# The last 64 tokens of local queries and keys: two full transpositions in place of four half ones

## The chip, the cores and the metric

The kernel runs on one core of a Trainium2 chip. The metric is the device time of one execution in microseconds. Five engines work beside each other, each through its own list of instructions: TensorE (PE for the matmuls, PEld for the weight loads that go before them), VectorE (DVE), ScalarE (ACT), GpSimd (POOL) and SyncE (SP), which here only starts DMA transfers. A transposition on TensorE is a matmul against an identity: the data is loaded as the weights, the identity is streamed, and the result lands in PSUM, from where ACT copies it to SBUF.

## The reference

Attention over 8 batches of 8 heads, 576 tokens of 64 values each, then a mixture of 8 experts over the 4608 tokens. Only the first step is touched by the change.

```python
scores = scale * np.matmul(q, k.transpose(0, 1, 3, 2))
rel = pos[:, None] - pos[None, :]
mask_local = (rel >= 0) & (rel < 32)                       # heads 0 to 3
mask_strided = (rel >= 0) & (rel % 32 == 0)                # heads 4 to 7
attn = softmax(where(mask, scores, -1e9))                  # per head
x = (attn @ v)  ->  (4608, 512)
e = argmax(x @ w_gate);  y = relu(x @ w1[e]) @ w2[e] * gate
```

## The kernel before, in words

The attention goes batch by batch. Heads 4 to 7 ("s", strided) and heads 0 to 3 ("l", local) alternate in a pipeline of 40 steps, five to a batch: `ch` lists them, and the loop over `n` writes the instructions of one step for every engine. Each engine runs its instructions in the order in which this loop wrote them. In step `n` the loads of the next batch are issued on SP, the transpositions for step `n + 3` are written (`tr`), the scores of step `n + 1` (`qks`, `qkl`), the softmax of step `n` and the products with the values of step `n - 2` (`avs`, `avl`).

The local queries and keys of a batch are loaded by `load_l`, 128 tokens at a time: `jj` runs over 0 to 4, and 576 = 4 x 128 + 64, so that the fifth piece has only 64 tokens. A piece is one DMA for q (tile `ql`) and one for k (tile `kl`): tokens on the partitions, the four heads one behind the other in the free dimension. `tl` transposes a piece: two heads (2 x 64 values) at a time, so four transpositions, two of `ql` (line 191) and two of `kl` (line 193), into one PSUM tile `t`; one ACT copy (line 194) brings them into `QK[b % 2]`, where the scores are taken from. For the fifth piece the four transpositions have 64 rows of tokens as input and 64 columns of output.

The order around it: `tl(b, 4)` stands at the start of a step, directly behind the value products `avl` (line 346) and ahead of the strided scores `qks` (lines 226, 231) and of the strided queries of the next batch (`ts`, line 203). On SP the loads of one batch come in the order q and k of the strided heads (`load_s`, lines 87 and 88, tiles `qs` and `ks`), local q and k (line 103), strided values (`load_vs`, line 93), local values (`load_vl`, line 112). Between them stand the stores of finished rows to `xrows` (line 381), each of which waits for ACT's copy into `xr`. For batches 0 and 1 nothing is stored yet. The DMAs of SP take turns on eight completion semaphores (DMAHW0 to DMAHW7 in the lists below): each DMA first waits until the one eight places ahead of it has landed. Names in the trace: buffers that lie inside other tiles show as `w` (strided keys and values of odd batches), `xg` (local values of odd batches) and `x` (`QK` of odd batches).

Of the kernel before, what the change touches and what calls it, by code (L numbers as in the profile page):

```python
# [12 lines left out]
AF = mybir.ActivationFunctionType  # L13
# [5 lines left out]
B, H, S, D = 8, 8, 576, 64  # L19
ST = 32  # L20
# [19 lines left out]
def kernel(ctx, tc, q, k, v, w_gate, w1, w2, out):  # L40
    nc = tc.nc
    V, A, G, T = nc.vector, nc.scalar, nc.gpsimd, nc.tensor
# [17 lines left out]
    ql, kl, vl, qs, ks, vs = {}, {}, {}, {}, {}, {}  # L60

    QK = [p0.tile([128, 2, 2, ST + S], F32, name="qk"),
          XA[:, :4 * (ST + S)].rearrange("p (w h s) -> p w h s", w=2, h=2)]
# [16 lines left out]
    def base(t, b, h):  # L80
        return t.offset + (b * H + h) * S * D
# [15 lines left out]
    def load_l(b, jjs=range(5)):  # L97
        for jj in jjs:
            for nm, src, dst in (("ql", q, ql), ("kl", k, kl)):
                if jj == 0:  # L100
                    dst[b] = ld.tile([128, 5, 4, D], F32, name=nm)
                n = 128 if jj < 4 else 64
                nc.sync.dma_start(dst[b][:n, jj], bass.AP(tensor=src.tensor, offset=base(src, b, 0) + jj * 128 * D,
                                                          ap=[[D, n], [S * D, 4], [1, D]]))

    def load_vl(b):
        t = VL[b % 2]
# [19 lines left out]
    ident = keep.tile([128, 128], F32)  # L127
    V.tensor_scalar(ident, jp, 0.0, None, op0=OP.is_equal)
    identb = const.tile([128, 128], BF)
    V.tensor_copy(identb, ident)  # L130
    load_s(0)
    load_l(0, (0, 1))

    rowq = const.tile([128, 1], F32)
# [50 lines left out]
    QTS, PS, PL, PT, OL, XS, XL, RL = ({} for _ in range(8))  # L185

    def tl(b, jj):
        n = 128 if jj < 4 else 64
        p = ps.tile([128, 4, 128], F32, name="t", bufs=3)
        for a in range(2):  # L190
            T.transpose(p[:, a, :n], ql[b][:n, jj, 2 * a:2 * a + 2, :], ident[:n, :n])  # L191
        for a in range(2):
            T.transpose(p[:, 2 + a, :n], kl[b][:n, jj, 2 * a:2 * a + 2, :], ident[:n, :n])
        A.activation(QK[b % 2].rearrange("p w h s -> p (w h) s")[:, :, ST + 128 * jj:ST + 128 * jj + n], p[:, :, :n], AF.Copy)
        yield

    def ts(b, w, x):
# [388 lines left out]
    src = keep.tile([TM, NC], I32, name="src")  # L586
# [88 lines left out]
    def tr(n):  # L675
        if not 0 <= n < N: return
        kd, b, i = ch[n]
        if n % 5 == 0:
            yield from ts(b, 1, 0)
            yield from ts(b, 1, 1)  # L680
            yield from ts_end(b)
        elif kd == "l":
            for jj in ((0, 1), (2, 3), (4,))[i]:
                yield from tl(b, jj)
            if i == 2 and b + 1 < B:
                yield from ts(b + 1, 0, 0)
                yield from ts(b + 1, 0, 1)
# [11 lines left out]
    def batch(n, d, f):  # L699
        if (n - d) % 5 == 4 and 0 <= (n - d) // 5 < B:  # L700
            return f((n - d) // 5)

    load_l(0, (2, 3, 4))
    load_vs(0)
    load_vl(0)
    for n in range(-1, N + 3):
# [5 lines left out]
        bb, m = n // 5 + 1, n % 5  # L712
# [3 lines left out]
        if bb < B:  # L716
            if m == 0 and n >= 0:
                if n == 0:
                    load_s(1)
                load_l(bb, (0, 1))  # L720
                if n == 0:
                    load_prev(0)
            if m == 1:
                load_l(bb, (2, 3, 4))
            if m == 2:
                load_vs(bb)
            if m == 3:
                load_vl(bb)
                if bb + 1 < B and n > 0:
                    load_s(bb + 1)  # L730
            if m == 4 and n > 0:
                load_prev(bb)
# [8 lines left out]
        if n == 1:  # L741
            nc.sync.dma_start(wg[:, :, :8], bass.AP(tensor=w_gate.tensor, offset=w_gate.offset,
                                                    ap=[[8, 128], [1024, 4], [1, 8]]))
# [54 lines left out]
    b = B - 1  # L798
# [298 lines left out]
    with tc.If(total > 0):  # L1097
# [10 lines left out]
        for e in range(E):  # L1108
            nc.sync.dma_start(f1, w1[e].rearrange("(c p) f -> p c f", p=128))
            nc.sync.dma_start(f2, w2[e].rearrange("(c p) d -> p c d", p=128))  # L1110
            n = nc.values_load(lvi[0:1, E + e:E + e + 1], min_val=0, max_val=NTOK)
# [56 lines left out]
```

## Time and profile before

| what | value |
|---|---|
| median of the runs shown (lowest, highest) | 663.3 us (662.58, 672.38), 3 runs |
| the profiled execution | 660.2 us, its span 658.4 us |
| PE busy over the span | 612.1 us (93%), 7502 matmuls |
| PEld busy | 542.1 us (82%) |
| DVE, ACT, POOL busy | 376.2, 323.6, 206.3 us |
| share of the last chain of work | PE 57%, issue 15%, SP's queue 8%, DVE 8%, ACT 6%, DMA 3% |

The profile is of one execution; 1.8 us of its 660.2 us lie outside the span from the first to the last instruction. The chain of work that ended last is followed back from the end, at each step to what released it; "issue" is time for which the profile shows no waited-for work. The attention takes the first 200 us or so, the experts the rest.

### The profile page before, as it was taken

What the parts mean: (1) busy time and instruction counts of PE and PEld (TensorE: products, weight loads), DVE (VectorE), ACT (ScalarE), POOL (GpSimd) and SP (SyncE); (2) the same over time, 40 slices, a digit from 0 to 9 for tenths busy, and PEclk for the clock granted to TensorE, in tenths of its full rate; (3) what the DMA queues carried; (4) which work ended last, traced back from release to release, by engine and by line L of the source; (5) the groups of instructions that cost most, each with busy time, mean ns of one, the idle gap of its engine ahead of it and who ended that gap; (6) DMA issues with size and microseconds to landing.
All of it is one profiled execution on the core that took longest, in us unless ns stands there. A gap on an engine that the chain in (4) does not pass through costs nothing.

```text
span 658.4 us, 18975 instructions
## 1 busy us (share of the span) xinstructions
PE 612.1 (93%) x7502; PEld 542.1 (82%) x7502; DVE 376.2 (57%) x834; ACT 323.6 (49%) x647; POOL 206.3 (31%) x347
## 2 busy tenths in 40 slices
PE   6689999988987889999999999999999999999995
PEld 4467676766755768999899999999999999999994
DVE  5767889878898653765445544644462752544200
ACT  6457766866764342544543543643642742534311
POOL 0222256436445681504304203403301600110212
PEclk9689999999997999999999999999999999999998
DMA  8997798879555277658978678868467867453111
GB/s 189 185 233 195 194 229 208 203 191 223 136 187 167 84 265 148 209 109 173 323 126 202 226 143 177 310 120 213 156 160 126 283 196 127 159 150 71 49 37 58
DMA packets 237955, 114.24 MB, mean 174 GB/s; under 512 B 209053, under 2 KB 211101, under 8 KB 237728
## 3 DMA queue, kind: packets, MB, share of 16 engines
q1 hardware_dynamic: 230096, 89.70, 56.9%
q0 software_dynamic: 7632, 22.03, 10.5%
q8 instruction: 79, 1.29, 0.9%
q14 instruction: 148, 1.21, 0.6%
HBM read 74.47 MB, written 21.83 MB: 146 GB/s over the span
## 4 chain that ended last, share of the span: by engine, by line
PE 57%; issue 15%; SPq 8%; DVE 8%; ACT 6%; DMA 3%; POOL 1%; POOLq 0%; ACTq 0%; DVEq 0%
PE h L642 6%; PE h L643 6%; PE h L644 6%; SPq L611 4%; PE y L918 3%; PE y L917 3%; PE y L919 3%; SPq L941 3%; PE o L346 2%; PE t L191 2%; PE o L275 2%; PE sc L298 2%; PE t L203 2%; PE t L328 2%; PE sc L231 1%
## 5 line engine op out<-in xcount | busy, mean ns | idle before, releaser
L649 DVE SCALAR_TENSOR_TENSOR h1l<-h,h1h 128x256 fp32r<-128x256 f32 (+3 forms) x64 | 32.5, 507 | 90.3 <-ACT h1h L648 85.4
L642 PE MATMUL h<-x,w1h 128*128 128x256 f32 (+3 forms) x256 | 81.0, 316 | 1.2 <-ACT yo L666 1.2
L644 PE MATMUL h<-x,w1l 128*128 128x256 f32 (+3 forms) x256 | 80.8, 316 | 0.0
L643 PE MATMUL h<-x,w1h 128*128 128x256 f32 (+3 forms) x256 | 80.8, 316 | 0.0
L917 PE MATMUL y<-h1h,w 128*128 128x256 f32 (+4 forms) x256 | 79.4, 310 | 1.4 <-ACT yt L924 1.4
L918 PE MATMUL y<-h1l,w 128*128 128x256 f32 (+4 forms) x256 | 79.5, 310 | 0.1
L919 PE MATMUL y<-h1h,w 128*128 128x256 f32 (+4 forms) x256 | 79.2, 309 | 0.0
L905 POOL DMA_INDIRECT out_dram<-yo,idx x16 | 15.8, 990 | 181.3 <-ACT yo L666 181.0
L642 PE MATMUL h<-x0h,w1h 128*128 128x256 f32 x224 | 63.5, 284 | 0.4 <-DVE h0l L649 0.4
L643 PE MATMUL h<-x0l,w1h 128*128 128x256 f32 x224 | 63.3, 283 | 0.0
L644 PE MATMUL h<-x0h,w1l 128*128 128x256 f32 x224 | 63.3, 283 | 0.0
L603 POOL DMA_INDIRECT xg<-xrows,src x48 | 52.9, 1101 | 30.0 <-issue 12.5
L905 POOL DMA_INDIRECT out_dram<-yq,idx x32 | 36.2, 1130 | 79.1 <-ACT yq L945 54.8
L648 ACT ACTIVATE h1h<-h 128x256 fp32r<-128x256 f32 (+3 forms) x64 | 28.5, 451 | 63.9 <-PE h L644 52.1
L575 DVE TENSOR_TENSOR w1l<-stg,w1h 128x1024 fp32r<-128x1024 f32 x32 | 37.8, 1227 | 33.0 <-ACT w1h L574 11.6
L649 DVE SCALAR_TENSOR_TENSOR h0l<-h,h0h 128x256 fp32r<-128x256 f32 x56 | 22.8, 420 | 49.8 <-issue 25.5
L642 PEld LDWEIGHTS h<-x,w1h 128*128 128x128 f32 x256 | 48.0, 188 | 2.0 <-ACT yo L666 1.7
L917 PEld LDWEIGHTS y<-h1h,w 128*128 128x128 f32 x256 | 48.1, 188 | 1.7 <-ACT yt L924 1.6
L918 PEld LDWEIGHTS y<-h1l,w 128*128 128x128 f32 x256 | 48.1, 188 | 0.4 <-DVE h1l L649 0.3
L643 PEld LDWEIGHTS h<-x,w1h 128*128 128x128 f32 x256 | 48.0, 188 | 0.3
L919 PEld LDWEIGHTS y<-h1h,w 128*128 128x128 f32 x256 | 48.2, 188 | 0.1
L644 PEld LDWEIGHTS h<-x,w1l 128*128 128x128 f32 x256 | 48.0, 188 | 0.0
(255 smaller groups left out, 1527.4 us busy)
## 6 DMA issues: line engine op xcount, KB each, us to landing
stg<-in_moe_w_dram SPq DMA_DIRECT2D x64, 512.0 KB
xr<-xg SPq DMA_DIRECT2D x112, 96.0 KB
xrows<-xr SPq DMA_DIRECT2D x16, 512.0 KB
yq<-yt SPq DMA_DIRECT2D x112, 64.0 KB
qs<-in_q_dram SPq DMA_DIRECT2D x8, 512.0 KB
ks<-in_k_dram SPq DMA_DIRECT2D x8, 512.0 KB
ql<-in_q_dram SPq DMA_DIRECT2D x32, 128.0 KB
kl<-in_k_dram SPq DMA_DIRECT2D x32, 128.0 KB
```

Source lines behind the costliest of these rows:

```text
L575: V.tensor_tensor(l[:, i], t, h[:, i].bitcast(F32), op=OP.subtract)
L603: G.indirect_dma_start(out=XG[t], out_offset=None, in_=x_out[:rows, :], in_offset=bass.IndirectOffsetOnAxis(ap=src[:, NT * e + t:NT * e + ...
L611: nc.sync.dma_start(XR[ST * q:ST * q + ST, a], rows[ST * a:ST * a + ST, :, q])
L642: T.matmul(p, W1H[:, c, fs], x[0][:, c, :n], start=(c == 0), stop=False)
L643: T.matmul(p, W1H[:, c, fs], x[1][:, c, :n], start=False, stop=False)
L644: T.matmul(p, W1L[:, c, fs], x[0][:, c, :n], start=False, stop=(c == 3))
L648: A.activation(h[0][:, f, :n], p, AF.Relu)
L649: V.scalar_tensor_tensor(h[1][:, f, :n], p, 0.0, h[0][:, f, :n].bitcast(F32), op0=OP.max, op1=OP.subtract)
L905: i = G.indirect_dma_start(out=out, out_offset=bass.IndirectOffsetOnAxis(ap=idx[:r, c:c + 1], axis=0), in_=YO[t][:r], in_offset=None, boun ...
L917: T.matmul(p[:, :n], W2H[:, f, ds_], H1[0][:, f, cs], start=(f == 0), stop=False)
L918: T.matmul(p[:, :n], W2H[:, f, ds_], H1[1][:, f, cs], start=False, stop=False)
L919: T.matmul(p[:, :n], W2L[:, f, ds_], H1[0][:, f, cs], start=False, stop=(f == 7))
```

## The change

The fifth piece is laid out otherwise: heads 0 and 1 of the 64 tokens lie on partitions 0 to 63, heads 2 and 3 on partitions 64 to 127. So it takes two DMAs for q and two for k, 64 tokens by two heads each, instead of one and one with four heads, and one transposition of 128 rows for q and one for k instead of two and two of 64 rows. The result in PSUM has the same columns in the same order, now without gaps between them; the ACT copy reads the same number of elements. All else stays.

```diff
@@ load_l
-                n = 128 if jj < 4 else 64
-                nc.sync.dma_start(dst[b][:n, jj], bass.AP(tensor=src.tensor, offset=base(src, b, 0) + jj * 128 * D,
-                                                          ap=[[D, n], [S * D, 4], [1, D]]))
+                if jj < 4:
+                    nc.sync.dma_start(dst[b][:, jj], bass.AP(tensor=src.tensor, offset=base(src, b, 0) + jj * 128 * D,
+                                                             ap=[[D, 128], [S * D, 4], [1, D]]))
+                else:
+                    for a in range(2):
+                        nc.sync.dma_start(dst[b][64 * a:64 * a + 64, jj, :2],
+                                          bass.AP(tensor=src.tensor, offset=base(src, b, 2 * a) + jj * 128 * D,
+                                                  ap=[[D, 64], [S * D, 2], [1, D]]))
@@ tl
-        n = 128 if jj < 4 else 64
+        n, m = (128, 2) if jj < 4 else (64, 1)
         p = ps.tile([128, 4, 128], F32, name="t", bufs=3)
-        for a in range(2):
-            T.transpose(p[:, a, :n], ql[b][:n, jj, 2 * a:2 * a + 2, :], ident[:n, :n])
-        for a in range(2):
-            T.transpose(p[:, 2 + a, :n], kl[b][:n, jj, 2 * a:2 * a + 2, :], ident[:n, :n])
-        A.activation(QK[b % 2].rearrange("p w h s -> p (w h) s")[:, :, ST + 128 * jj:ST + 128 * jj + n], p[:, :, :n], AF.Copy)
+        for w, x in enumerate((ql, kl)):
+            for a in range(m):
+                T.transpose(p[:, m * w + a], x[b][:, jj, 2 * a:2 * a + 2, :], ident)
+        A.activation(QK[b % 2].rearrange("p w h s -> p (w h) s")[:, :, ST + 128 * jj:ST + 128 * jj + n],
+                     p[:, :2 * m].rearrange("p x (y t) -> p (x y) t", t=n), AF.Copy)
```

PE, the fifth piece of batch 1, before: it stands behind the value products of batch 0.

```order
L346 MATMUL o<-vl,ptl 32x64 x16
L191 MATMUL t<-ident,ql 128x64 [waits DMAHW2_49,Activation_49]
L191 MATMUL t<-ident,ql 128x64
L193 MATMUL t<-ident,kl 128x64 [waits DMAHW3_49]
L193 MATMUL t<-ident,kl 128x64
L226 LDWEIGHTS identb
```

The same place on PE after the change (line numbers are five or six higher).

```order
L351 MATMUL o<-vl,ptl 32x64 x16
L197 MATMUL t<-ident,ql 128x128 [waits DMAHW5_49,DMAHW4_49,Activation_49]
L197 MATMUL t<-ident,kl 128x128 [waits DMAHW7_49,DMAHW6_49]
L231 LDWEIGHTS identb
L231 MATMUL sc<-mks,identb 128x144 [waits DVE_49]
```

Two matmuls and their weight loads are gone, and each of the two that are left waits for two DMAs. Over the whole program PE's list is 16 matmuls shorter.

SP at the start of the program, before: from the fifth piece of batch 0 to the strided queries of batch 1, the last row.

```order
L103 DMA ql<-in_q_dram 64x4x64 [waits DMAHW4_49]
L103 DMA kl<-in_k_dram 64x4x64 [waits DMAHW5_49]
L93 DMA vs<-in_v_dram 18x4x512 [waits DMAHW6_49,DVE_49]
L93 DMA vs<-in_v_dram 18x4x512 [waits DMAHW7_49]
L93 DMA vs<-in_v_dram 18x4x512 [waits DMAHW0_49]
L93 DMA vs<-in_v_dram 18x4x512 [waits DMAHW1_49]
L112 DMA vl<-in_v_dram 32x18x64 [waits DMAHW2_49]
L112 DMA vl<-in_v_dram 32x18x64 [waits DMAHW3_49]
L112 DMA vl<-in_v_dram 32x18x64 [waits DMAHW4_49]
L112 DMA vl<-in_v_dram 32x18x64 [waits DMAHW5_49]
L87 DMA qs<-in_q_dram 128x1024 [waits DMAHW6_49]
```

The same stretch on SP after, up to the last of the local values; the strided queries of batch 1 follow with a wait on DMAHW0.

```order
L107 DMA ql<-in_q_dram 64x2x64 [waits DMAHW4_49]
L107 DMA ql<-in_q_dram 64x2x64 [waits DMAHW5_49]
L107 DMA kl<-in_k_dram 64x2x64 [waits DMAHW6_49]
L107 DMA kl<-in_k_dram 64x2x64 [waits DMAHW7_49]
L93 DMA vs<-in_v_dram 18x4x512 [waits DMAHW0_49,DVE_49]
L93 DMA vs<-in_v_dram 18x4x512 [waits DMAHW1_49]
L93 DMA vs<-in_v_dram 18x4x512 [waits DMAHW2_49]
L93 DMA vs<-in_v_dram 18x4x512 [waits DMAHW3_49]
L117 DMA vl<-in_v_dram 32x18x64 [waits DMAHW4_49]
L117 DMA vl<-in_v_dram 32x18x64 [waits DMAHW5_49]
L117 DMA vl<-in_v_dram 32x18x64 [waits DMAHW6_49]
L117 DMA vl<-in_v_dram 32x18x64 [waits DMAHW7_49]
```

Two transfers more stand ahead of the values, so the semaphore on which each later DMA waits belongs to a transfer two places further on. Two are added per batch, 16 in all, and 16 is twice around the eight semaphores: from the first load of expert weights on, SP's list and its waits are the same as before.

## Rows read from the trace of the kernel before

**Rows 1.** Busy time by stretch: length, engines (count), PE's clock, DMA share, GB/s.

```profile
0.00:200.00 200.00, 171.83 (x4565) 127.70 (x4567) 159.13 (x459) 135.23 (x297) 79.15 (x178) 0.96 0.82 197
240.00:659.00 419.00, 406.81 (x2620) 387.11 (x2618) 186.76 (x285) 173.47 (x322) 101.19 (x125) 0.99 0.64 165
```

**Rows 2.** What PE waited for, 0 to 200 us: total, times, longest.

```profile
PE t L203 <- DMA qs<-in_q_dram: 9.7, 2, 5.3
PE o L346 <- issue: 5.1, 6, 1.6
PE sc L231 <- issue: 2.8, 1, 2.8
```

**Rows 3.** Groups by form, 0 to 200 us: busy us, mean ns | idle before.

```profile
L191 PE MATMUL t<-ident,ql 64*128 64x64 f32 x16 | 2.7, 248 | 0.0
...
L193 PEld LDWEIGHTS t<-ident,kl 64*128 64x128 f32 x16 | 1.6, 139 | 0.0
```

**Rows 4.** Timeline of PE, 30 to 60 us: start, length of the merged group.

```profile
31.55 0.44 PE L191 MATMUL t<-ident,ql 128*128 128x128 f32 x2
31.82 0.38 PE L193 MATMUL t<-ident,kl 128*128 128x128 f32 x2
...
41.64 0.34 PE L191 MATMUL t<-ident,ql 64*128 64x64 f32 x2
...
42.03 0.30 PE L226 MATMUL sc<-mks,identb 128*128 128x144 bf16 x2
...
53.26 0.33 PE L218 MATMUL t<-ident,qs 128*128 128x128 f32 x1
...
53.63 0.72 PE L275 MATMUL o<-w,w 128*64 128x72 f32 x16
```

**Rows 5.** Semaphore instructions of PE's queue at lines 191 and 218: count, ns.

```profile
L191 PEldq EVENT_SEMAPHORE  x40: 51/51/332, 8.2 to 184.5; - x40
L218 PEldq EVENT_SEMAPHORE  x8: 51/51/51, 7.3 to 170.1; - x8
```

**Rows 6.** Timeline of SP's queue, 8 to 20 us.

```profile
9.00 0.77 SPq L103 DMA_DIRECT2D ql<-in_q_dram  x1
...
10.54 1.58 SPq L93 DMA_DIRECT2D vs<-in_v_dram  x4
```

**Rows 7.** The last chain within 0 to 30 us: start, length, what.

```profile
8.45 4.50 DMA kl<-in_k_dram
...
13.86 2.70 SPq L112
...
16.61 6.77 DMA qs<-in_q_dram
```

**Rows 8.** Busy time in a stretch of the start, columns as in rows 1.

```profile
11.00:14.00 3.00, 2.54 (x76) 2.00 (x76) 1.06 (x3) 2.91 (x7) 0.00 (x0) 1.00 0.60 128
```

**Rows 9.** Timeline of SP's queue, 20 to 200 us, loads for batches 1 and 2.

```profile
27.14 0.51 SPq L103 DMA_DIRECT2D kl<-in_k_dram  x1
27.69 0.61 SPq L103 DMA_DIRECT2D ql<-in_q_dram  x1
...
29.05 0.55 SPq L742 DMA_DIRECT2D wg<-in_moe_w_gate_dram  x1
...
35.35 1.76 SPq L87 DMA_DIRECT2D qs<-in_q_dram  x1
```

**Rows 10.** Around PE's pause at 42.7 us: timeline, and DMA queues 42 to 46 us.

```profile
45.46 0.26 PE L231 MATMUL sc<-w,qts 128*18 128x36 f32 x8 [2.80 <-issue]
45.65 1.12 PE L203 MATMUL t<-ident,qs 128*128 128x128 f32 x4
...
q8 instruction: 1, 0.02, 2.0%
```

**Rows 11.** Timeline of SP's queue, 20 to 200 us, a later batch.

```profile
119.67 1.80 SPq L93 DMA_DIRECT2D w<-in_v_dram  x4
124.64 0.51 SPq L381 DMA_DIRECT2D xrows<-xr  x1
```

## The prediction

> **What bounds the kernel now.** I read the busy time by stretch first. The attention, some 200 us, has PE busy 172 us of 200; the experts, 419 us, have it busy 407 [rows 1]. The change touches no instruction of the second stretch, and there PE has no idle time that a transfer could open or close, so whatever the attention gains or loses is handed on to the end as it is. The question is only what the attention's PE stream does.
>
> Second, what PE waits for in the attention [rows 2]. The reader is to see two things. One wait is for data: 5.3 us for the strided queries of batch 1, once (the other 4.4 us of that row is the start of the program). The others are called "issue": 2.8 us in the middle of a run of line 231, 5.1 us in six pieces in the middle of runs of line 346. Nothing that the program orders ends them. The longest sits between two matmuls of one group, and in its 4 us the only packet outside the load queue is one of an instruction queue, 0.02 MB [rows 10]; I infer, without proof, that PE is waiting for its own code behind a busy DMA. The half transpositions themselves have 0.0 us of idle time before them [rows 3]. They are thus plain work in PE's stream: they count for what they occupy there, and for nothing more.
>
> Third, SP's queue, because the change adds to it. From the first load to the loads of batch 2 it issues almost without a gap, and the chain of waits runs through it: a load that lands 4.50 us after its issue, one issue of 2.70 us, and 6.77 us from the issue of batch 1's strided queries to their landing, when PE goes on [rows 7].
>
> **The change part by part.**
>
> *PE, eight times.* Four half transpositions take 0.39 us from the first start to the start of what follows (41.64 to 42.03) [rows 4]. For two full ones there are two rows to go by. At line 191 the first pair of a four-piece transposition takes 0.27 us to the next start (31.55 to 31.82). At line 218 one transposition of q and one of k, each with its own DMA to wait for, take 0.37 us (53.26 to 53.63) [rows 4]. This second row has the form that the change makes: two single transpositions from two tiles, with another kind of matmul behind. I take it: 0.39 - 0.37 = 0.02 us a batch, 0.2 us in all. The best case is 8 x 0.12 = 1.0 us. The worst comes from the waits: at both lines a matmul with two or three waits has one semaphore instruction of 51 ns in front (40 for 40 pieces, 8 for 8) [rows 5]. The transposition of k now waits for two DMAs where it waited for one, so a second such instruction comes in. As PE's sequencer runs ahead I take it as hidden; if not, it makes 0.37 into 0.42, and the term turns to a loss of 8 x 0.03 = 0.2 us.
>
> Why so little for half the instructions: the half ones are cheap. Weight loads of 64 rows last 139 ns each [rows 3], yet the whole four are through in 0.39 us, so they overlap each other.
>
> On weight loads the Trainium skill (TensorE: Matmul & The Clock Gate, LDWEIGHTS) says that a load's time is set by its columns and not by its rows, so that a half transposition pays for a full one's load; two loads less a batch would by that be worth twice the load. The duration agrees, but that four follow each other in 0.39 us speaks against the conclusion; it stands below as a rival.
>
> *ACT.* The copy has 128 x 256 elements before and after; nothing.
>
> *SP, start of the program.* For batch 0 the two loads of the fifth piece hold the queue from 9.00 to 10.54, 1.54 us [rows 6]. What a load of 64 tokens by two heads costs to issue is not in the trace. Nearest are the piece of 128 tokens by four heads, 0.51 us, and of 64 by four, 0.61 us [rows 9]; half the partitions did not make it cheaper, so I do not let half the heads do so either, and take 0.51 us and the 0.04 us between issues: 4 x 0.55 = 2.2 us, 0.7 us more. Behind these stand the values, and behind them batch 1's strided queries, for which PE idles 5.3 us. Does the delay reach them? The values must still wait for the last 128-token piece of k, which lands 4.50 us after 8.45, at 12.95 [rows 7]; before, one load of values was out of SP by then and three were left up to the long issue at 13.86. Afterwards the third load of strided values is out, and one strided and three local ones stand ahead of the last: two more issues, 0.8 us. If the long issue keeps its 2.70 us, the queries land 0.8 us later. It is long because the DMA engines are full at that time; between 11 and 14 us they were only 0.60 busy [rows 8], so bytes that come later there are really lost time. I take 0.8 us; the ends are 0 (the long issue shortens by what it started later) and 1.7 us (each of the four as long as the 0.77 us row [rows 6]: 4 x 0.81 - 1.54).
>
> By the Trainium skill (DMA: Bandwidth & Descriptors, Rules for kernel authors) two transfers to disjoint halves of the partitions are not worth it, since both spread over the same engines one after the other, and one of 128 partitions is to be used; it also calls transfers under 64 KB mostly overhead, and these are 32 KB. If each costs as much as the 64 KB one, 0.61 us, the term is 4 x 0.65 - 1.54 = 1.1 us in place of 0.7, and the sum 0.3 to 0.4 us higher.
>
> *SP, batch 1.* Again two issues more (27.69 to 29.05 before), and the queue runs gapless from there to batch 2's strided queries at 35.35 [rows 9]. PE takes these at 45.65 [rows 10]. Ten microseconds are more than the 6.77 that batch 1's took [rows 7], so the cover is 3.5 us and holds: 0. If not, up to 0.8 us.
>
> *SP, batches 2 to 7.* The extra issues delay the values by some 0.8 us, and right after these SP stands idle until ACT has filled a row to store: 119.67 + 1.80 = 121.47, next issue at 124.64, 3.2 us [rows 11]. The wait swallows it. The pieces themselves are loaded most of a batch ahead of their use. Cost 0; the list of SP in the experts is unchanged.
>
> *The pauses of PE.* Later loads and a shorter list move the "issue" pauses about. I see no direction in that: 0, with the longest, 2.8 us [rows 2], as the bound on either side.
>
> Sum: -0.2 + 0.8 + 0 + 0 = +0.6 us, so 660.8 us against the profiled execution's own 660.2. That execution lies 3.1 us below the median of the runs shown, 663.3, and 2.4 below their lowest; put on the median, the time is **663.9 us**.
>
> **The rivals.**
>
> *The weight loads set PE's pace.* Then each batch is relieved of two loads of 139 ns [rows 3]: 8 x 0.28 = 2.2 us, and with the start hidden 663.3 - 2.2 = 661.1 us. For it: PEld is busy 128 of the attention's 200 us beside PE [rows 1]. Against it: the four half loads that overlap. This is what the rule of the Trainium skill on weight loads, above, would give. Chance 0.12.
>
> *The longest pause goes.* If the shift of the loads takes the 2.8 us pause out, the time is 663.9 - 2.8 = 661.1 us. For it: it hangs on a packet that met a burst of loads. Against: PE and the loads shift together. Chance 0.1.
>
> *SP's extra issues reach PE in every batch*, slower than before. The place is the load queue between the fifth piece and the next strided queries; it decides if SP's idle time at line 381 is less than 0.8 us in each batch. Price 8 x 0.8 = 6.4 us, less 0.2: 669.5 us. Against it: 3.2 us of idle time a batch. A weaker form is that batch 1 pays too or that a pause grows: 663.9 + 0.8 to + 2.8, 664.7 to 666.7. Chance 0.08 for the full one, 0.2 for the weak one.
>
> *The change does nothing on PE and the start is hidden*: 663.3 us, inside the forecast's own range. It shares the forecast's 0.5.
>
> **How the numbers follow.** Forecast and "nothing" 0.5, around 663.3 to 664.4; faster by 2 to 3 us 0.22; slower by 1 to 3 us 0.2; slower by 6 us 0.08. The range takes in the two faster cases (661.1, and less if both come) and the weak slower one, and leaves out the full slower one and what lies beyond both: 660.3 to 667.5. The runs of before alone spread from 662.6 to 672.4. A change of 2% is 13 us, about what a measurement of this kernel can tell from none; not even the full slower rival gets there, nor all the pauses gone and the first rival together (2.8 + 5.1 us [rows 2] and 2.2 us). So within 2% 0.97, slower 0.02 for stalls that pile up, faster 0.01.
>
> **What would show it.** In the profile after: at the new lines 197 two matmuls a batch with 0.34 to 0.42 us to the next start, where 0.27 would be the best case; 16 matmuls and weight loads fewer; eight more semaphore instructions there. At the start the strided queries of batch 1 landed at about 24.2 us instead of 16.61 + 6.77 = 23.4. Four issues of 0.4 to 0.6 us a batch on SP, and the idle time before line 381 shorter by as much. PE's waits in the experts the same. I would be wrong if the small loads landed so late that a transposition waited for them, or if the pauses of PE changed by more than all the terms here.

## The result, and the profile after

The changed kernel takes 671.5 us (median of 5 runs, 670.72 to 676.75) against 665.3 us for the kernel before (5 runs, 662.58 to 672.38). The ratio is 1.012, 95% interval 1.0081 to 1.0159: slower, and 4.0 us above the top of the predicted range. Ratios here and below are over the runs of the chip's faster state alone, so they need not be the quotient of the two medians. The profiled executions lie further apart, 669.6 us of span against 658.4. That of before lies below the five timed runs; a second profile of the changed kernel (below) has 667.0. So what the two profiles show is some 11 us, of which the medians bear out 6 to 8.

Where it lies is read first from busy time by stretch, after; the columns are those of rows 1. The first stretch has 16 matmuls fewer than that of before and is its counterpart.

```profile
0.00:210.00 210.00, 177.67 (x4549) 132.46 (x4551) 159.31 (x460) 135.58 (x297) 79.86 (x179) 0.92 0.79 188
251.00:670.00 419.00, 406.77 (x2616) 387.93 (x2614) 186.55 (x285) 172.84 (x321) 101.14 (x125) 0.99 0.64 163
```

The experts are as they were: 419 us with 406.8 busy [rows 1]. The attention is 10 us longer, in two parts: PE idles 32.3 us instead of 28.2 (+4.2), and is busy for 177.7 instead of 171.8 (+5.8) although it has less to do, at a granted clock of 0.92 instead of 0.96.

The idle part, by what PE waited for in the first 210 us after (total, times, longest), to be set beside rows 2:

```profile
PE t L208 <- DMA qs<-in_q_dram: 11.2, 2, 6.8
PE o L351 <- issue: 5.0, 3, 1.9
PE sc L236 <- issue: 3.0, 2, 2.4
PE sc L231 <- DVE w L258: 1.9, 1, 1.9
...
PE sc L231 <- DVE mxs L257: 1.6, 1, 1.6
PE o L280 <- issue: 1.5, 1, 1.5
...
PE sc L303 <- issue: 0.9, 1, 0.9
```

The wait for batch 1's strided queries grew by 1.5 us. The pauses called "issue" grew too: those over 0.2 us up to the last batch (nine before, from the 2.80 us of rows 10 on, and nine after) add up to 8.7 us before and to 13.9 after, if the two rows at line 231 with DVE as releaser are counted. I count them because they stand where the list puts a pause: 0.90 and 1.57 us before, at the end of the products of line 346, now a few matmuls further on, as each batch took two matmuls and two loads out of the list and put one semaphore instruction in. Counted in the traces with weight loads and semaphore instructions, the two places are instructions 3778 and 7362 of PE's list before, 3777 and 7362 after. Without them the sum after is 10.4 us. In the second profile of this kernel pauses stand at the same two places, and the first is put down to another DVE instruction; its sum is 12.7 us. So the growth is 4 to 5 us, from one profile of before and two of after.

The timeline of PE after shows the transpositions, a pause and the clock behind it (start, length of the group, and in brackets the idle time ahead):

```profile
25.37 1.09 PE L208 MATMUL t<-ident,qs 128*128 128x128 f32 x4 [6.75 <-DMA qs<-in_q_dram]
...
44.09 0.33 PE L197 MATMUL t<-ident,ql 128*128 128x128 f32 x1
44.25 0.27 PE L197 MATMUL t<-ident,kl 128*128 128x128 f32 x1
44.36 0.29 PE L231 MATMUL sc<-mks,identb 128*128 128x144 bf16 x2
44.58 0.44 PE L236 MATMUL sc<-w,qts 128*18 128x36 f32 x27
47.45 0.31 PE L236 MATMUL sc<-w,qts 128*18 128x36 f32 x5 [2.43 <-issue]
...
50.99 1.11 PE L369 MATMUL t<-ident,xr 128*128 128x128 f32 x4
```

Two full transpositions take 44.36 - 44.09 = 0.27 us to the next start; the same at 119.77 and 194.34. Behind the pause the four transpositions of line 369 take 1.11 us; four at full clock take 0.66. Busy time in the stretch behind the pause, after:

```profile
48.00:52.00 4.00, 4.00 (x61) 3.07 (x60) 1.81 (x5) 1.97 (x4) 0.00 (x0) 0.50 0.95 231
```

Clock 0.50 is the lower of the two levels, 1.2 GHz; before, the same stretch held 101 matmuls at 0.86. The clock fell behind the pause of before too (four transpositions at 45.65 take 1.12 us [rows 10]), but there four take 0.70 us again at 48.94, where after the change they still take 1.06 us at 52.75. A pause thus costs more than its own length, and not in proportion to it: this one is the shorter of the two, 2.43 us against 2.80.

SP's queue at the start, after (start, length of the merged issues):

```profile
8.75 1.42 SPq L107 DMA_DIRECT2D ql<-in_q_dram  x2
10.21 1.26 SPq L107 DMA_DIRECT2D kl<-in_k_dram  x2
11.59 1.57 SPq L93 DMA_DIRECT2D vs<-in_v_dram  x4
```

The values start at 11.59 instead of 10.54 [rows 6]. A half-size load holds the queue as long as the whole one: the 16 of q last 601 to 1592 ns, median 613, and a whole one took 0.61 us in rows 9. The chain of waits over the first 32 us, after:

```profile
17.51 7.73 DMA qs<-in_q_dram
```

Issued 0.90 us later than before and 0.96 us slower on its way [rows 7], the tile lands at 25.24 instead of 23.38.

SP's queue in the later batch, after, beside rows 11:

```profile
123.33 2.24 SPq L107 DMA_DIRECT2D ql<-in_q_dram  x2
125.61 1.27 SPq L107 DMA_DIRECT2D kl<-in_k_dram  x2
126.99 0.53 SPq L386 DMA_DIRECT2D xrows<-xr  x1
127.62 1.81 SPq L93 DMA_DIRECT2D w<-in_v_dram  x4
131.23 0.52 SPq L386 DMA_DIRECT2D xrows<-xr  x1
```

From 129.43 to 131.23 SP is idle, 1.8 us where it was 3.2. The wait did swallow the extra issues, just as forecast, and still time was lost in nearly every batch. The first transposition of the second local piece marks the batches (line 191 before, 197 after, the one that waits 0.3 to 0.4 us for ACT): 55.25, 77.89, 101.16, 123.81, 148.39, 172.72 before; 3.3, 5.1, 6.6, 6.6, 8.9 and 9.6 us later after.

### The profile page after: what moved, and what is told of

It reads as the page before. It is cut to its first block, busy times and chain, and to the rows that moved or that the text cites. A ratio compares the mean times of both kernels' runs of the same rounds, so it can differ in the third digit from the quotient of the medians.

```text
span 669.6 us, 18967 instructions
## 1 busy us (share of the span) xinstructions
PE 618.8 (92%) x7486; PEld 548.3 (82%) x7486; DVE 376.1 (56%) x834; ACT 324.1 (48%) x647; POOL 207.4 (31%) x347
## 4 chain that ended last, share of the span: by engine, by line
PE 60%; issue 14%; SPq 7%; DVE 7%; ACT 5%; DMA 4%; POOL 1%; POOLq 0%; ACTq 0%; DVEq 0%
PE h L647 7%; PE h L649 7%; PE h L648 7%; PE y L922 4%; PE y L923 4%; PE y L924 4%; SPq L616 3%; PE t L197 3%; PE o L351 2%; DMA xg<-xrows,src 2%; PE t L208 2%; SPq L946 2%; PE sc L303 2%; PE o L280 2%; PE t L333 2%
## 5 line engine op out<-in xcount | busy, mean ns | idle before, releaser
L647 PE MATMUL h<-x0h,w1h 128*128 128x256 f32 x224 | 63.5, 283 | 0.0
L922 PEld LDWEIGHTS y<-h1h,w 128*128 128x128 f32 x256 | 48.8, 191 | 3.2 <-ACT yt L929 3.1
L924 PEld LDWEIGHTS y<-h1h,w 128*128 128x128 f32 x256 | 48.9, 191 | 0.0
```

Of the source, the lines that this page charges most:

```text
L647: T.matmul(p, W1H[:, c, fs], x[0][:, c, :n], start=(c == 0), stop=False)
L922: T.matmul(p[:, :n], W2H[:, f, ds_], H1[0][:, f, cs], start=(f == 0), stop=False)
L924: T.matmul(p[:, :n], W2L[:, f, ds_], H1[0][:, f, cs], start=False, stop=(f == 7))
```

## The experiments

Three theories at first. A: more and later loads make the pauses of PE longer; the pauses are PE waiting for its own code behind data. B: PE's shorter list or its full transpositions are to blame. C: it is the start of the program alone, carried along. Every ratio is against the kernel before, on the same chip. Totals of PE's "issue" waits in this part are as the profile labels them, over the first 212 us: 9.2 us before, 10.4 after.

**The loads alone.** The fifth piece is loaded by four transfers, but to the old places; PE keeps its four half transpositions.

```diff
-                nc.sync.dma_start(dst[b][:n, jj], ...ap=[[D, n], [S * D, 4], [1, D]]
+                    for a in range(2):   # jj == 4
+                        nc.sync.dma_start(dst[b][:64, jj, 2 * a:2 * a + 2], ...ap=[[D, 64], [S * D, 2], [1, D]]
```

> The fifth piece is loaded with two DMAs for q and two for k, as in the change, but into the old layout (64 partitions, four heads), and PE keeps its four half transpositions. Theory A (the 16 further DMA issues on SP put the loads later against PE, and PE's pauses grow by it): 7 to 11 us slower than before, the pauses called issue at 13 to 15 us in the attention against 8.7. Theory B (PE's shorter list moves the places at which PE pauses, and the loads do not matter): within 2 us of before. Theory C (only the start pays, 1.9 us and what a colder clock adds): 2 to 4 us slower.

671.76 us, ratio 1.0076 (1.0041 to 1.0111). What PE waited for, first 205 us of this run:

```profile
PE o L351 <- issue: 7.9, 5, 2.2
PE o L280 <- issue: 2.6, 2, 1.4
PE sc L236 <- issue: 2.5, 1, 2.5
```

The pauses grow to 14.2 us with the old transpositions. The loads carry most of the loss, some 5 us; A gains, though it had expected 7 to 11.

**The transpositions alone.** Two full transpositions of a piece that one transfer fills: 128 tokens of heads 0 and 1. The last 64 tokens of heads 2 and 3 are left out, and tokens 448 to 511 of heads 0 and 1 stand in their place.

```diff
+                    nc.sync.dma_start(dst[b][:, jj, :2],   # jj == 4
+                        ...offset=base(src, b, 0) + (jj * 128 - 64) * D, ap=[[D, 128], [S * D, 2], [1, D]]
```

> Two full transpositions for the fifth piece, as in the change, but fed by one DMA for q and one for k of the same bytes as before: 128 tokens of heads 0 and 1 in place of 64 tokens of four heads. It leaves out the last 64 tokens of heads 2 and 3 (other values stand there). SP's list is as before. Theory A: about 1 us faster than before (8 x 0.12). Theory B: 5 to 9 us slower, as in the change. Theory C: about 1 us faster.

664.14 us, ratio 0.9961 (0.9924 to 0.9998). Theory B falls: without the extra transfers the full transpositions lose nothing, and gain by a little more than the noise. The 2.6 us (0.1 to 5.1 by the interval) take in PE's own 8 x 0.12 = 1.0 us; the piece is also loaded onto twice the partitions, so this run does not say if there is more to it.

**Batches 0 and 1 alone, batches 2 to 7 alone.** Both layouts stand in the kernel, chosen by batch.

```diff
+                if not (jj == 4 and b < 2):    # the old load; the new one otherwise, and so in tl
```

> The change in batches 0 and 1 alone, batches 2 to 7 as before. Theory A: 3 to 4 us slower, and the later pauses about as before. Theory C: 7 to 10 us slower, as much as the whole change, since all that follows is set off by the late start. Theory B: anything, since PE's list is shorter by eight instructions only.

665.6 us, ratio 1.002 (0.9985 to 1.0054). The other way round, `b > 1`:

> The change in batches 2 to 7 alone, batches 0 and 1 as before. Theory A: 4 to 7 us slower. Theory C: 0 to 1 us faster, since the start is as before. The forecast's own step (SP's idle time swallows the later issues): 0 to 1 us faster.

667.59 us, ratio 1.003 (0.9996 to 1.0064). Theory C falls: the start alone gives nothing to speak of. But A's own sizes are missed as well, 3 to 4 us and 4 to 7 us slower where the ratios make 1.3 and 2.0. Neither half can be told from no change, so these runs don't say in which batches the loss arises; together they give 0.5% where the whole gives 1.0 to 1.2%, and the intervals don't say if halves add up.

**The changed kernel again**, unchanged, timed beside the others.

> The changed kernel once more, as a measure beside the ones that follow. By the two halves measured apart (loads alone 1.0076, PE's form alone 0.9961) it would be at 1.004 if they simply add; by its first measurement at 1.012.

671.02 us, ratio 1.0096 (1.0061 to 1.0131): it repeats, somewhat smaller, and nearer to the first measurement than to the 1.004 of the two parts added up. Why the whole should cost more than its parts is not shown; their intervals are too wide to say that it does.

**The fifth piece loaded later**, behind the next strided tiles.

```diff
             if m == 1:
-                load_l(bb, (2, 3, 4))
+                load_l(bb, (2, 3))
...
                     load_s(bb + 1)
+                load_l(bb, (4,))
```

> The changed kernel, but from batch 1 on the four loads of the fifth piece are issued behind the strided queries and keys instead of ahead of the values. Theory A1 (the four issues hold up the values and the strided loads behind them, and PE's code comes late behind these): at or below before, 0.994 to 1.000, with PE's pauses back to 8 to 10 us. Theory A2 (split transfers are slow wherever they stand): as the change, 1.004 to 1.012.

666.21 us, ratio 1.0003 (0.9977 to 1.0028). The "issue" waits shrink to 4.2 us, but another wait takes their place, at the fifth piece itself, which now lands too late for its transposition:

```profile
PE t L197 <- DMA ql<-in_q_dram: 3.2, 3, 2.2
```

The longest of the three, on PE's timeline:

```profile
46.29 0.30 PE L197 MATMUL t<-ident,ql 128*128 128x128 f32 x1 [2.15 <-DMA ql<-in_q_dram]
```

This is the wait that the prediction named as a sign of being wrong; the changed kernel itself does not show it. With the loads at another place the changed kernel is level with the one before. It is not their number as such that made it slower.

**Batch 1's strided tiles ahead of batch 0's values**, in the kernel before.

```diff
     load_l(0, (2, 3, 4))
+    load_s(1)
     load_vs(0)
...
-                if n == 0:
-                    load_s(1)
```

> The kernel before, with the strided queries and keys of batch 1 loaded ahead of the values of batch 0. It tells whether PE's wait of 5.3 us at the start and the half clock behind it are set by what stands ahead in SP's queue: if so, 4 to 7 us faster (0.990 to 0.994); if the values are then late for the local heads, no gain, and PE waits at the value products instead.

664.5 us, ratio 0.9957 (0.992 to 0.9994). The start's wait is worth something, less than the expected 0.990 to 0.994, as part of it comes back under another name:

```profile
PE sc L290 <- DVE w L241: 6.1, 3, 5.0
```

**Slots without bytes.** The kernel before with three transfers of 64 bytes behind the fifth piece of every batch.

```diff
+                for i in range(3):
+                    nc.sync.dma_start(tiny[:, bb, i], bass.AP(tensor=q.tensor, ...ap=[[D, 1], [1, 16]]))
```

> The kernel before with three further DMAs of 64 bytes a batch behind the fifth piece, which nobody uses: some 1.0 us of SP's time a batch, nearly no bytes. Theory A1: 2 to 5 us slower, pauses longer. Theory A2: within 1 us of before.

667.66 us, ratio 1.003 (0.9999 to 1.006). Three such issues last 1.06 us in batch 1, about what the change adds. The "issue" waits are 12.5 us, so pure delay of SP's queue can lengthen them, but the time says at most a part of the loss.

**The fifth piece behind the strided values.** The changed kernel, with these four loads moved by one place in the list from batch 1 on.

```diff
             if m == 1:
-                load_l(bb, (2, 3, 4))
+                load_l(bb, (2, 3))
             if m == 2:
                 load_vs(bb)
+                load_l(bb, (4,))
```

> The changed kernel with the four loads of the fifth piece behind the strided values instead of ahead of them, from batch 1 on: in SP's stretch of idle time before the store at line 381, a place where nothing of SP's is held up. Theory A1 (what stands behind them is late): 0.994 to 1.000 of before. Theory A2 (split loads cost wherever they stand): 1.004 to 1.012.

661.9 us, ratio 0.9935 (0.9899 to 0.9971): faster than before, clock 0.980. SP's queue in the later batch of this run:

```profile
122.26 1.87 SPq L93 DMA_DIRECT2D w<-in_v_dram  x4
124.18 2.09 SPq L107 DMA_DIRECT2D ql<-in_q_dram  x2
126.31 1.26 SPq L107 DMA_DIRECT2D kl<-in_k_dram  x2
127.68 0.54 SPq L386 DMA_DIRECT2D xrows<-xr  x1
128.33 3.73 SPq L117 DMA_DIRECT2D xg<-in_v_dram  x4
```

The values go out 5.4 us earlier than after the change (122.26 against 127.62), but 3.6 of these are the whole program being ahead (the batch's marker stands at 126.81 instead of 130.40); against the batch they are 1.8 us earlier. SP's queue has no idle time before the store. The pauses over 0.2 us, by place as above, add up to 9.5 us instead of 13.9. Its control is the kernel before with its two loads at that same place (the same diff):

> The control for the first of these: the kernel before with its two loads of the fifth piece behind the strided values. If the place alone is worth something: 0.994 to 0.998. If the place only matters for the split loads: 0.999 to 1.002.

668.43 us, ratio 1.0021 (0.9983 to 1.006). The place alone gains nothing for the old layout, although the values leave early in all batches here too; the pauses by place are 11.5 us. So the new layout, at this place, is worth 0.9% (1.0021 to 0.9935).

**That place and the start together**: the change, the fifth piece behind the values, batch 1's strided tiles first (the two diffs above).

> The same, and the strided queries and keys of batch 1 ahead of batch 0's values. If the gains add (0.9957 was measured for the second edit on the kernel before): 0.990 to 0.996, faster than both kernels.

660.47 us, ratio 0.9887 (0.9849 to 0.9925). The lowest time of all, and better than both kernels; its interval overlaps that of the version without the second edit (0.9899 to 0.9971).

**The strided values later, nothing else.** The kernel before; no transfer and no byte more. It tests theory A in a sharper form, A1: what counts is how late the values' bytes are, since they then share the DMA engines with the strided tiles of the next batch and with PE's code.

```diff
-            if m == 2:
-                load_vs(bb)
             if m == 3:
+                load_vs(bb)
                 load_vl(bb)
```

> The kernel before with the strided values of the next batch loaded one step later, directly ahead of the local values: no DMA more, no byte more, only 0.6 MB that go out some 5 us later and meet the strided queries and keys. Theory A1 in its sharper form (SP's idle time is time in which the DMA engines work off what was issued, so bytes that come later stand in front of the strided loads and of PE's code): 3 to 8 us slower, with longer pauses of PE. If only SP's own time counted: no slower, since SP issues no more than before.

678.49 us, ratio 1.0189 (1.0136 to 1.0242): a larger loss than the change's, without a line of the change. What PE waited for, first 210 us of this run:

```profile
PE t L203 <- DMA qs<-in_q_dram: 11.2, 4, 6.0
PE o L346 <- issue: 8.5, 5, 4.7
PE sc L231 <- issue: 2.8, 2, 2.5
PE t L203 <- issue: 2.3, 1, 2.3
PE sc L298 <- issue: 2.0, 3, 1.0
```

"Issue" is 16.5 us. The longest one, on PE's timeline of this run:

```profile
98.08 0.31 PE L346 MATMUL o<-vl,ptl 64*32 64x64 f32 x1 [4.72 <-issue]
```

And the same matmul, the last of the same run of 32, in the kernel before:

```profile
90.88 0.24 PE L346 MATMUL o<-vl,ptl 64*32 64x64 f32 x1 [0.90 <-issue]
```

Same instruction, same list on PE; only loads on another engine have moved, and the pause is five times as long.

How far this run goes beyond the change is seen from SP's queue in the later batch:

```profile
139.54 1.59 SPq L93 DMA_DIRECT2D w<-in_v_dram  x4
```

The marker of that batch stands at 138.11, so the values leave 1.4 us behind it, where they left 4.1 us ahead of it before (119.67 and 123.81). For batches 2 to 7, us ahead of the marker:

| batch | 2 | 3 | 4 | 5 | 6 | 7 |
|---|---|---|---|---|---|---|
| before | 3.5 | 3.4 | 4.4 | 4.1 | 3.9 | 4.4 |
| after | 4.5 | 3.4 | 4.4 | 2.8 | 3.2 | 4.4 |
| after, fifth piece behind the values | 4.0 | 4.4 | 4.5 | 4.6 | 4.4 | 5.0 |
| before, values later | -1.5 | -1.4 | -1.4 | -1.4 | -1.4 | -1.4 |

The change itself delays the values of two of these batches, by 1.4 and 0.8 us (of three in its second profile, by 0.8 to 1.1 us); this run delays all six by 5 to 6 us. It shows that late values lengthen the pauses and cost time. That the change's own loss comes about in this way is not shown by it.

**PE's list moved by 40 matmuls.** The kernel before with 40 small matmuls and their weight loads at the front of PE's list. If the pauses are the fetching of code, they stay at the same count from the list's start and so move 40 matmuls back in the program.

```diff
     load_l(0, (2, 3, 4))
+    for _ in range(40):
+        T.matmul(SC[:32, 0, 0, :32], identb[:, :32], identb[:, :32], start=True, stop=True)
```

> The kernel before with 40 small matmuls and their weight loads put in front of PE's list, where PE has nothing to do for 4.4 us anyway: 80 instructions more ahead of everything. If the pauses called issue are PE waiting for its own code, they sit at fixed distances along the list and move 80 instructions towards the start of the program: the one with 7 of 32 matmuls of a value product left would come 40 matmuls sooner, so with 47 or more still to come (in the local scores or transpositions ahead of it), while the times of the loads stay. If they are something of the instruction itself, they stay at 7, 1, 11, 6 and 18 matmuls left. Time within 4 us of before either way, since the loads are untouched.

663.46 us, ratio 0.9986 (0.9944 to 1.0029). In the kernel before, PE's timeline has a pause in the middle of the products of batch 1:

```profile
65.30 0.43 PE L346 MATMUL o<-xg,ptl 64*32 64x64 f32 x25
66.16 0.31 PE L346 MATMUL o<-xg,ptl 64*32 64x64 f32 x7 [0.43 <-issue]
```

In this run it stands in the scores ahead of them:

```profile
65.43 0.42 PE L298 MATMUL sc<-qk 64*32 64x64 f32 x22
67.35 0.33 PE L298 MATMUL sc<-qk 64*32 64x64 f32 x10 [1.50 <-issue]
```

Between the two places are 10 + 4 + 25 = 39 matmuls. Counted from the start of the list the pause stays where it was. Busy time from the program's start to the pause, before:

```profile
0.00:66.00 66.00, 49.62 (x1233) 37.47 (x1233) 44.52 (x129) 41.09 (x85) 15.92 (x36) 0.90 0.90 201
```

And with the 40 in front:

```profile
0.00:67.00 67.00, 50.78 (x1234) 38.48 (x1234) 43.37 (x127) 40.70 (x83) 16.09 (x36) 0.90 0.90 197
```

1233 and 1234 matmuls. The changed kernel has 1232 at its pause of 70.57, the run with the late values 1233. The pause of 90.88 stands at 1867 before, 98.08 of the late values at 1867, 97.06 of the changed kernel (one of the two with the DVE label) at 1864, as its list has fewer matmuls and more semaphore instructions up to there. With weight loads and semaphore instructions counted in, the pauses of before stand at 1473, 2498, 2754, 3778, 5058, 5826, 6082, 7362 and 9153 of PE's list: 256 apart or a multiple of it, to within one. In the run with 40 in front they stand at 1473, 2498, 3777, 5058, 6337 and 7361.

## Why the prediction was wrong, step by step

**The failed step is the one on the pauses**: "The pauses of PE ... I see no direction in that: 0", with 2.8 us as the bound on either side, and with it "The wait swallows it. ... Cost 0" for the loads of batches 2 to 7. The pauses grew by 5.2 us in one profile and by 4.0 in the second, past that bound and past all other terms, which the prediction itself gave as a sign of being wrong. The lower clock behind such waits has no term in the sum at all: by the rows above it held back 0.04 of 200 us before and 0.08 of 210 after, by estimate some 9 us more of full clock. SP's idle time ahead of the store did swallow the issues, and the argument stopped there, at the queue.

What the runs show in its place: the extra loads lose time with PE's list as before (1.0076), and the changed kernel loses by the place of these loads, since it is faster than before when they alone are moved (1.012 and 1.0096 against 0.9935). How they lengthen the pauses is in part argued. While SP waited, the DMA engines could work off the values; with the values later, these are still under way when the strided tiles of the next batch and PE's code come. That late values lengthen the pauses was shown by moving them alone (1.0189), but by four times the delay of the change or more. And batches 2 to 7 alone gave 1.003, which can't be told from nothing: the step failed in what it left out of the account, and how much of the loss arises in these batches stays open.

The pauses were called PE's code behind a busy DMA "without proof". Their place in the list settles it as far as these runs can: they follow the count of instructions and not the program, and their length follows the loads. The packet of an instruction queue passes once ahead of each pause that I looked at, 2.1 to 3.1 us before its end (taken by windows of half a microsecond). DMA queues of the kernel before, 63.5 to 64.0 us (PE goes on at 66.16):

```profile
q8 instruction: 1, 0.02, 13.8%
```

And after, 68.0 to 68.5 us (PE goes on at 70.57):

```profile
q8 instruction: 1, 0.02, 13.4%
```

Set against the issue of that batch's strided queries, for this one pause, the packet passes 3.5 us behind it before (60.24 to 63.75, the middle of its window), 5.9 us after (62.33 to 68.25), 6.0 us with the loads alone and 3.4 us with the piece behind the values.

The pauses stand 127 matmuls or a multiple apart ((1867 - 1233) / 5 = 126.8), and 256 of all of PE's instructions. The Trainium skill (Runtime: NRT & Kernel Launch, Instruction fetch mechanics) says that instructions are refilled in blocks of 16 KiB, 256 of them, by the engine's own DMA queue, and that the cost of a block's boundary is mostly hidden. Spacing (127 matmuls with their loads are 254, the semaphore instructions aside) and packet size agree. Mostly hidden holds by number, with 36 packets of that queue and nine pauses over 0.2 us in the first 200 us before; what is left is not small, 8.7 us there and up to 4.72 us for one in the run with the values later.

**PE: -0.2 us forecast, -1.0 measured, if all batches are like the three that show it** (0.39 to 0.27 us at 44.09, 119.77 and 194.34). In two others the pair takes 0.48 us at the lower clock, and in the other three a wait or a pause stands inside it. Of the two rows I took the slower; the faster one, 0.27 us, "the best case", came true. The reason for the choice, two tiles with a wait each, was not what made the 0.37: the extra semaphore instruction is there (below) and costs nothing. What made it, no run shows. The queue of PE at line 197, 8 more than the 40 of rows 5:

```profile
L197 PEldq EVENT_SEMAPHORE  x48: 51/51/302, 7.9 to 194.2; - x48
```

**The start: +0.8 us forecast, +1.9 measured in the first profile, +0.9 in the second** (PE goes on at 25.37 and 24.41 us instead of 23.52). An issue of half the heads costs 0.61 us and not 0.51: the four hold the queue from 8.75 to 11.59, 1.3 us more than the two did, and as the queue came to them 0.25 us sooner, the values left 1.05 us later, not 0.7. The estimate that went by the rule of the Trainium skill on small transfers (DMA: Bandwidth & Descriptors, Rules for kernel authors), 1.1 us, came nearer than mine, and the trace agrees with the rule as far as half the bytes took as long to issue. In the first profile the long issue did not shorten (2.83 us against 2.70), and the transfer took 0.96 us more. That is just above the stated end of 1.7, but five profiles with the old start scatter from 23.51 to 24.34 us, so the forecast of 0.8 is not refuted.

**Batch 1: 0 forecast; the cover held.** The strided queries of batch 2 were issued at 38.00 us instead of 35.35 and taken at 47.70 instead of 45.65; no wait for data stands there, a pause of 2.43 us does.

**The rivals.** The weight loads do not set PE's pace: 1.0 us, not 2.2. The longest pause did not go, it became 2.43. "SP's extra issues reach PE in every batch" came nearest, with 6.4 us against 6.2 of the medians, but by another way, so that the size agrees by chance: its condition, less than 0.8 us of idle time on SP, was not met (1.8 us were left). Its weaker form, "that a pause grows", with a chance of 0.2, had the right mechanism and was too small: not one pause but the sum of them grew, and the clock fell behind some.

The account of the two profiles, then: 4.2 us more idle time in the attention (pauses +5.2, the start's wait +1.5, others less), and 5.8 us more busy time, which I put down to the lower clock behind those waits, less up to 1.0 us that the transpositions save; 1.2 us lie behind it, ahead of the experts.

**Open.** How the loss divides between slots in SP's queue (1.003 for slots alone, which can't be told from nothing) and the smaller transfers (1.0076 for the loads; their bytes and the 256 bytes of a row are as before). Whether the delay of the values by the change, small as it is, sets the length of its pauses. Why the new layout gains 0.9% at the better place, some 5.7 us, where PE's own share is at most 1.0 us. When PE asks for its code: no row shows the request, only the packet.

## What to carry to other kernels

Idle time of a queue that starts transfers need not be a cover: ask what its bytes do in that time, and who needs the DMA engines next. A long list of small matmuls fetches its own code over the same engines; pauses called "issue" at even distances in the list are that, and here their length changed with the order of the loads. A layout that loses at one place in the load order (1.012) may win at the next (0.9935): move the loads before giving up the layout.

## What was unexpected on the chip

A pause for code lasted 4.72 us with the strided values loaded one step later, and 0.90 us at the same instruction in the kernel before. Moving these values, with no byte added, cost 1.9%, some 12 us; the "issue" waits rose by 7.3 us (9.2 to 16.5), and the mean granted clock of the profiled execution was 0.962 against 0.981. Over the runs the clock goes with the time: 0.980 in the run of 661.9 us, 0.970 with the loads alone, 0.963 after the change. Whether pauses of PE alone lower it, no run separates.
